# A fused attention and feed-forward kernel: loads of q and k in pairs, a new written-out order, and the norm's reciprocal root moved from VectorE to GpSimd

## The chip, the cores and the metric

One core of one Trainium2 chip runs the whole program. The metric is the device time in microseconds of one execution, the median over runs. The engines are TensorE (PE; its weight loads are listed apart as PEld), VectorE (DVE), ScalarE (ACT), GpSimd (POOL, which also makes the descriptors of the DMAs that it issues) and SyncE (SP, which here only issues DMAs). Matrix products land in eight PSUM banks of 128 x 512 fp32.

## The reference

Attention with a window of 128 keys and 4 sink keys over 4 batches, 8 heads, 768 positions, head size 64; then an RMS norm over the 512 features of each of the 3072 tokens and a SwiGLU feed-forward layer of width 1536.

```python
scores = (q @ k.T) / sqrt(64)             # per batch and head
keep   = is_sink | (0 <= i - j < 128)     # 4 sink keys, window of 128
a      = softmax(where(keep, scores, -1e9))
x      = (a @ v), heads side by side      # 3072 x 512
rms    = sqrt(mean(x * x, axis=-1) + 1e-6)
xn     = x / rms * rms_g
g      = xn @ w_gate                      # 512 x 1536
out    = ((g * sigmoid(g)) * (xn @ w_val)) @ w_out
```

Inputs and output are fp32; the kernel computes in bf16 with fp32 sums.

## The kernel before

The 3072 tokens are 24 blocks of 128, numbered g = 0 to 23, six to a batch (t = g mod 6). Six groups G of four blocks go through the feed-forward layer.

**One block of attention.** POOL issues three loads for each block (q, k, v: `load_bf16`, L353, and `load_v`, L357), which cast to bf16 on the way; only q and k of block 0 come as fp32 through SP and are cast by ACT (L349). For blocks 0 to 7 PE transposes q and k (`pe_t`, L445, four 128-column transposes for each), and DVE or ACT copies the result into the tile `qkT` (`copy_t`, L452); from block 8 on SP does it with a transposing DMA (`dma_t`, L459). Scores are computed transposed, keys on partitions: a block's keys against the queries of the same block (n = 0) and of the next (n = 1). Blocks 0, 1, 2, 3 and the first of each batch use `scores` (L485): eight products of 256 columns into four banks, one for each half of the heads and each of `u`; blocks 0 and 1 do it in two parts of eight products of 128 columns (`SPLIT`). Blocks with t = 1 to 4 from block 4 on use `tri_scores` (L563, 24 products of 64 x 64 tiles), the last of a batch `scores_last` (L501). Blocks 0 and 1 are masked on PE by a product that writes a bias first (`mask_bias`, L467), later ones after the exponential, on DVE (L547, L584, L520) or, from block 16, on POOL (L597, L526). ACT takes the exponentials (L536, L572, L512). `av` (L606 to L621) multiplies with the values; a column of ones in `V16` gives the denominators. `normal` (L660, L661, DVE) divides, `square` (L669, ACT) sums the squares into `ms`.

**The norm.** `rms` (DVE) turns `ms` into the reciprocal root by six operations on 128 x 1 (L676, L680 and four at L689) and then scales the block by it and by the gain `gb` (L693), giving `xr`. The constant C3 that these six leave over is folded into `gb` (`scale_gb`, L431). `xr` is transposed into `xnt`, for blocks 0 to 7 by PE (`pe_x`, L708) and a copy (L714), later by an SP DMA (`dma_x`, L720).

**The feed-forward layer.** A chunk is one bank of `g` (L975 with wg) and one of `u` (L975 with wv), `tanh` on ACT (L982), `silu` (L988) and `hidden` (L998) on DVE. Group 0 has chunks of 128 tokens and four 128-wide pieces of d_ff, groups 1 and 2 of 256 tokens, the rest of 512. `project` (L1008) multiplies with w_out, ACT evacuates (L1016), SP stores (L1020). The last 128 rows are done by `project_end` (L1028) in two pieces, 384 and 128 columns; ACT evacuates and stores the first, DVE and SP the second.

**What sets the order.** Nothing is decided at run time. Every operation is handed to a plan under a number; the table `ORDER` lists the numbers for each engine, `TURNS` how the engines' lists interleave as the program is written down, and `BANKS` the PSUM bank for each product. Each engine then works through its list strictly in that order and waits where an input is missing. Priorities and due times in the calls (`prio`, `gate_of`, `LOAD_LEAD`) were used to make the tables and do nothing any more once they stand. 56 small products of zeros (`warm`, L421) are part of PE's list; all stand within its first 22 us. POOL keeps at most eight loads in flight: each issue waits until the eighth load before it has landed.

Below, g(G, f, c) and u(G, f, c) name the two halves of the chunk of group G that starts at piece f and token c; s.3 stands for the scores of block 3, av.3 for its product with the values, xr.3, ms.3, qT.3, kT.3 for its tiles.

Of the kernel before, what the change touches and what calls it, by code (L numbers as in the profile page):

```python
# [9 lines left out]
ALU = mybir.AluOpType  # L10
# [9 lines left out]
C3 = -5.0 / 16.0  # L20
T1 = 2.5258847276
TP = T1 - 4.2
TQ = 7.0 / T1
# [48 lines left out]
140 138 114 151 122 152 124 143 154 119 156 157 117 111 142 173 171 153 127 133 118 163  # L72
135 169 149 112 198 123 174 179 167 165 186 136 141 148 200 134 125 129 184 164 121 161
120 131 202 128 139 221 146 203 208 240 144 162 223 213 190 215 155 137 115 194 113 225
596 145 147 159 132 150 597 166 160 242 219 232 126 234 158 130 611 116 601 612 616 238
602 631 617 606 626 621 607 259 622 244 627 632 636 251 277 253 261 637 263 196 666 656
279 661 257 281 269 651 271 646 294 641 319 657 647 286 658 288 296 652 642 321 298 662
275 663 323 671 292 305 672 307 681 667 676 331 329 668 673 677 311 691 339 315 686 682
696 354 687 697 335 347 345 692 701 369 706 317 360 362 707 702 384 736 375 716 711 737
721 377 738 712 726 398 717 727 389 741 391 742 417 731 722 751 746 743 752 405 407 747  # L80
732 761 756 762 753 757 776 425 748 766 423 771 767 772 777 432 781 816 782 817 447 791
796 438 440 792 806 786 818 797 787 801 462 821 455 811 802 453 807 822 471 473 823 493
831 826 812 827 832 484 828 486 500 512 833 502 836 846 837 851 847 861 841 876 842 852
862 521 866 856 871 857 523 881 867 877 872 891 530 886 882 887 896 892 897 548 898 921
541 922 539 926 936 916 906 566 907 927 559 908 557 937 946 584 917 575 931 941 947 589
577 932 951 942 901 952 956 966 902 991 903 986 971 591 961 911 987 912 972 967 913 957
992 996 1001 962 1006 1002 1007 1021 1011 993 981 997 976 1012 1016 988 1022 982 1026
983 1036 1031 1017 1046 1037 1061 1032 1051 977 1052 1047 1066 978 1027 1041 1056 1042
1057 1067 1058 1062 1068 1063 1071 1074
""",  # L90
    "ACT": """
24 20 22 199 177 175 178 176 182 180 181 183 168 188 222 204-206 211 207 212 209 191 210
217 226 228 227 229 195 598 220 236 603 613 618 608 243 633 628 260 623 245 247 246 248
638 278 262 255 264-267 197 280 282 284 653 273 320 648 643 295 297 659 290 322 299 301
300 302 276 324 325 293 326 327 309 664 678 669 683 674 333 312 693 340 316 341 688 342
343 698 355-357 336 358 703 370 371 708 372 318 373 349 385 364 387 718 713 723 739 379
399 401 400 402 728 418 419 733 420 393 421 409 763 758 778 768 754 773 744 749 427 433
414 783 434-436 448 449 793 450 798 451 442 808 788 819 803 463-466 813 457 824 480 475
482 494 496 497 495 513 488 514 515 504 834 838 516 848 843 853 829 863 868 858 878 873
525 883 531-533 893 509 888 534 899 923 549-551 928 552 938 543 567-569 918 570 585 587  # L100
933 943 948 561 953 579 958 909 904 968 593 963 914 973 1008 1003 994 998 1013 1028 1023
989 1038 1018 1033 984 1053 1048 1043 979 1069 1059 1064 1072 1073
""",
    "DVE": """
0 2 7 1 3 6 11 10 14 172 170 13 12 187 4 185 193 201 189 192 241 224 214 216 314 218 230
231 233 235 599 237 600 239 604 605 614 5 619 615 620 609 634 610 629 624 625 630 249
250 252 254 639 640 256 268 258 635 270 283 285 272 654 274 649 644 287 289 650 655 413
645 291 303 313 304 306 308 328 310 332 679 330 684 680 334 694 689 685 344 699 690 700
346 348 695 359 704 361 363 709 374 710 705 350 719 386 376 714 378 724 715 388 365 720
390 404 729 392 380 730 403 725 508 422 408 734 406 735 394 764 410 759 765 760 426 412  # L110
769 424 779 774 770 428 775 784 780 785 437 794 439 441 795 452 809 789 799 800 790 443
804 456 805 454 810 814 472 474 458 476 815 498 485 499 487 501 503 489 507 505 849 839
840 844 850 854 855 845 864 522 869 865 859 524 860 879 870 880 874 875 884 526 885 894
889 890 895 924 540 925 542 929 939 919 560 930 558 544 920 576 934 590 940 935 944 949
945 578 562 950 954 955 959 580 592 969 594 970 960 964 974 975 1009 965 1004 1010 999
1000 1014 1005 1015 1029 1024 1025 1019 1020 1034 1039 1040 1035 1049 1054 1055 1050
1030 1044 1045 1075
""",
    "POOL": """
25 8 9 26-28 31 34 30 32 37 35 29 38 33 39 41 42 40 43 45 47 44 48 46 49 36 50 53 57 52  # L120
54 51 56 63 62 60 55 58 64 61 59 65-99 467 469 468 470 481 100 483 101-108 517 520 109
518 519 535 538 537 536 110 553 555 554 571 573 556 572 588 586 574
""",
    "SP": """
19 21 23 16 15 18 17 337 352 338 353 367 660 382 368 383 396 415 397 416 430 675 351 445
366 431 460 446 381 670 665 478 740 395 479 411 492 745 461 510 491 429 755 511 528 444
459 750 477 506 564 582 546 529 565 490 820 547 835 527 830 583 825 545 563 581 595 915
905 910 900 995 990 980 985 1070 1060 1065 1076
# [3 lines left out]
ASDDSDGDPDPSPDPPPPPGPPPGPDPGPPDDPGAGPPPPADGPPPPGPPSPDPSADPGSDPSPGAAAPAGPAPPDAPPGPPAPDPAP  # L132
PPPADPGPDAGPPDPPDGAPPGPAPPAGDPAPAPDGADAPDGPAPPPADPAGPDAPADAGPPPPAPADGAPADGPPPPPAPPDPGPPD
DPAGPDPAGPDPGAPDDGPDGPDADGDPDGPADADPGAADPGPGDPADGAPDPGADAPGADADPGDPAPPDAPPDADAPGDPPADAGP
AAGPAPDAPPDPADPDAPGDAPDDGDPAPGDPPGSAAPGADAPGDPDGPPPDAGDAPGDADPPGADPAGDSAPPAGASPADPADSADP
PPGADAPGPSADDPGASAPGDPGSAPPGDPSADGAPDASDAPPDADPAGPPSAAADPAADPADPDAPAGADPGADPPDAPPADDPDGS
PDAPASAGDPPAPAGDSPADAPADDPPAGSADPPDASDPAGPADPSDDPGAPDDPADAPDGSDPDGPAGAPADSAPPADSDPPDGPDS
PDAGASPAAPDASGDPADSPDSDPGSPPPDDPSDGPDADPAPADPSDPSPDPSPDDAPDPDAPADPADAPDADAPDPDPASAPDASAP
DSADPADPDPASAPASADPAPPDASDPDAPSDASPADPDADPDPDPDAPASAPPDASADPAGPDGPGDPDGAPDPDPDPDAPAAGPSA
DGPAASGPADSPAGDPPGDDPGPPDGPDAAGPPDAGADPAGPAAGDPADAGPGPDSPGDPDASGPDGAADSPDAPDSDPPDSPDAPDS  # L140
ADPDSAPPDSDPSDAPDASPADDPDPDPADAPAAPDASADPADSPGSDGPDGSPGPGPAPAPADPAPDADPADAPDAGAPDGPGPAAP
AAPPADGDPPDGPDGDGPPAAPDSPGDPGAGPDAPPDPDPDPDAADPADPDDPAPAADPSDPDPDDPAAPPSPDDPAAPDPPSPPDPA
PSDSDSPASDPDPPPAAPDDPDPDPPAAPSDPDPAPDDPDPPPPAAPDADPSDPAAPDPDPAAPDDPDPDAPADPDPDPDPPDPAAPD
SPSDPPPPPAAPSASSPAADS
"""
BANKS = """
# [9 lines left out]
def kernel(  # L156
# [44 lines left out]
    POOL_MASK_FROM = 16  # L201
    X_DMA_FROM = 8
    QK_DMA_FROM = 8
    LD = 16
    GATE_FROM = 8
    LOAD_LEAD = 10
    LEAD_FROM = 10
# [222 lines left out]
    def scale_gb():  # L430
        nc.scalar.mul(gb, BANK.pop(("gb",)), C3)  # L431
# [709 lines left out]
```

## Time and profile before

| | before |
|---|---|
| median of 3 runs | 241.71 us (241.56 to 242.35) |
| profiled execution, first to last instruction | 241.9 us |
| its distance to the median of the runs | 0.2 us above |
| PE busy | 231.3 us (96%) |
| DVE busy | 187.4 us (77%) |
| ACT busy | 122.8 us (51%) |
| POOL busy | 89.2 us (37%) |
| granted PE clock | 1.00 |
| DMA packets | 113741, of which 103857 under 512 B |
| the queue of POOL's loads | 13.90 MB, 79.3% of the 16 DMA engines' time |

The profile is of one execution; PE is busy nearly throughout, and its products overlap in the pipeline, so a single product's duration (0.2 to 0.4 us) is longer than the time from one start to the next. The text takes the time from start to start wherever work is summed. The idle time of an engine is listed with what ended it.

### The profile page before, as it was taken

Reading aid. Unit: us, or ns where it says so; the run is one execution under the profiler, and the core shown is the slowest. Engines: PE = TensorE matmul, PEld = TensorE weight load, DVE = VectorE, ACT = ScalarE, POOL = GpSimd, SP = SyncE. Lnnn points to the kernel's source line nnn. Section 1 sums busy time; section 2 is a strip of 40 time slices with the busy share of each in tenths; the row PEclk is TensorE's granted clock in tenths of the full one; section 3 lists DMA queues with packets and bytes.
Section 4 is the critical chain, followed back from the end, with each engine's and each line's share of the span. In section 5 each row is a group of like instructions: output and inputs, shape, how many; then the busy total and the mean of one; then the engine's idle time right before and its main releaser. Section 6 shows DMA issues by size and latency. Waiting matters only on the chain.

```text
span 241.9 us, 5897 instructions
## 1 busy us (share of the span) xinstructions
PE 231.3 (96%) x2329; PEld 147.6 (61%) x2354; DVE 187.4 (77%) x478; ACT 122.8 (51%) x267; POOL 89.2 (37%) x116
## 2 busy tenths in 40 slices
PE   7889999999879999999999999999999999999995
PEld 5568986876668776777876644445554444444443
DVE  3599989989979999999898989994569946537520
ACT  4776368667766574337654464454543321233112
POOL 8985894597526554000004982022540000000000
PEclk9999999999999999999999999999999999999999
DMA  9999999999999999999601999527010114101024
GB/s 128 143 183 195 182 178 194 162 143 139 137 151 152 138 143 154 132 233 156 126 2 24 119 150 123 131 70 128 3 23 0 32 36 173 43 0 47 0 87 173
DMA packets 113741, 27.42 MB, mean 113 GB/s; under 512 B 103857, under 2 KB 110769, under 8 KB 113714
## 3 DMA queue, kind: packets, MB, share of 16 engines
q0 software_dynamic: 81760, 13.90, 79.3%
q1 hardware_dynamic: 31810, 12.95, 29.8%
q8 instruction: 18, 0.29, 0.5%
q10 hardware_dynamic: 144, 0.20, 0.2%
q14 instruction: 9, 0.07, 0.1%
HBM read 28.35 MB, written 6.29 MB: 143 GB/s over the span
## 4 chain that ended last, share of the span: by engine, by line
PE 67%; DMA 20%; POOL 6%; issue 2%; DVE 2%; SPq 2%; POOLq 0%
PE v L975 20%; PE o L1008 20%; PE g L975 18%; DMA wo<-in_moe_w_out_dram 5%; DMA qkT<-q 4%; DMA wv<-in_moe_w_val_dram 4%; DMA wg<-in_moe_w_gate_dram 3%; DMA q<-in_q_dram 3%; POOL v L357 2%; SPq L459 2%; PE s L563 2%; PE av L621 2%; POOL k L353 1%; PE av L616 1%; PE o_last L1028 1%
## 5 line engine op out<-in xcount | busy, mean ns | idle before, releaser
L975 PE MATMUL v<-xnt,wv 128*128 128x128 bf16 (+2 forms) x527 | 72.2, 282 | 0.4 <-DMA wv<-in_moe_w_val_dram 0.2
L975 PE MATMUL g<-xnt,wg 128*128 128x128 bf16 (+2 forms) x521 | 71.3, 281 | 0.4
L1008 PE MATMUL o<-wo,hT 128*128 128x512 bf16 x259 | 65.3, 379 | 1.1 <-issue 0.5
L982 ACT ACTIVATE th<-g 128x512 bf16<-128x512 f32 x72 | 41.7, 599 | 48.4 <-PE g L975 48.2
L988 DVE SCALAR_TENSOR_TENSOR p<-th,g 128x512 bf16<-128x512 bf16 x72 | 48.1, 682 | 18.9 <-ACT th L982 18.7
L975 PEld LDWEIGHTS <-wv 128*128 128x128 bf16 x528 | 43.3, 98 | 21.3 <-DMA wv<-in_moe_w_val_dram 0.6
L998 DVE TENSOR_TENSOR hT<-p,v 128x512 bf16<-128x512 bf16 x72 | 48.1, 682 | 9.3 <-PE v L975 7.8
L975 PEld LDWEIGHTS <-wg 128*128 128x128 bf16 x528 | 42.8, 98 | 19.3 <-issue 1.0
L1008 PEld LDWEIGHTS <-hT 128*128 128x128 bf16 x276 | 25.4, 98 | 26.5 <-issue 0.2
L597 POOL TENSOR_SCALAR_AFFINE_SELECT e<-e 128x512 bf16<-128x512 bf16 x20 | 12.7, 656 | 54.4 <-ACT e L572 53.0
L572 ACT ACTIVATE e<-s 128x384 bf16<-128x384 f32 x52 | 23.1, 495 | 12.5 <-PE s L563 12.5
L1016 ACT ACTIVATE osb<-o 128x512 f32<-128x512 f32 x23 | 13.4, 597 | 21.8 <-PE o L1008 18.0
L357 POOL DMA_DIRECT2D v<-in_v_dram x24 | 21.3, 888 | 8.5 <-DMA q<-in_q_dram 3.8
L353 POOL DMA_DIRECT2D q<-in_q_dram x23 | 20.4, 891 | 9.9 <-DMA k<-in_k_dram 6.7
L353 POOL DMA_DIRECT2D k<-in_k_dram x23 | 20.4, 889 | 9.1 <-DMA v<-in_v_dram 4.5
L669 ACT ACTIVATE sq<-x 128x512 bf16<-128x512 bf16 x24 | 15.1, 631 | 14.8 <-DVE x L661 14.5
L661 DVE TENSOR_TENSOR x<-av,rden 128x256 bf16<-128x256 f32 x48 | 20.4, 424 | 1.7
L693 DVE SCALAR_TENSOR_TENSOR xr<-x,r,gb 128x512 bf16<-128x512 bf16 x24 | 18.7, 778 | 0.8
L621 PE MATMUL av<-v,e 128*128 128x65 bf16 x192 | 16.4, 193 | 0.3 <-DMA v<-in_v_dram 0.3
L536 ACT ACTIVATE e<-s 128x512 bf16<-128x512 f32 (+1 forms) x36 | 15.1, 519 | 1.6 <-PE s L485 1.5
L616 PE MATMUL av<-v,e 128*128 128x65 bf16 x160 | 14.8, 193 | 0.0
L621 PEld LDWEIGHTS <-e 128*128 128x128 bf16 x192 | 12.7, 97 | 2.8 <-DVE e L547 0.4
(78 smaller groups left out, 192.6 us busy)
## 6 DMA issues: line engine op xcount, KB each, us to landing
out_dram<-osb SPq DMA_DIRECT2D x23, 256.0 KB, 2.2
v<-in_v_dram POOLq DMA_DIRECT2D x24, 128.0 KB, 8.9
q<-in_q_dram POOLq DMA_DIRECT2D x23, 128.0 KB, 8.1
k<-in_k_dram POOLq DMA_DIRECT2D x23, 128.0 KB, 9.6
wo<-in_moe_w_out_dram POOLq DMA_DIRECT2D x2, 768.0 KB, 11.3
wg<-in_moe_w_gate_dram POOLq DMA_DIRECT2D x5, 256.0 KB, 8.0
wv<-in_moe_w_val_dram POOLq DMA_DIRECT2D x5, 256.0 KB, 8.9
stage<-in_k_dram SPq DMA_DIRECT2D x1, 256.0 KB, 3.0
```

The lines of the kernel that those rows point to most:

```text
L353: nc.gpsimd.dma_start(out=T[name, g], in_=block_of(src, g))
L357: nc.gpsimd.dma_start(out=V16[b][:, t, :, 0:D], in_=block_of(v, g))
L572: nc.scalar.activation(out=e_tile(g)[:, x:x + 2, 0:TW], in_=BANK.pop(("s", g, u, hi))[:, 0:2 * TW].rearrange("p (j c) -> p j c", c=TW), fu ...
L616: nc.tensor.matmul(out=dest, lhsT=T["e", g - 1][:, x, P:2 * P], rhs=V16[b][:, t - 1, h, :], start=(t == 1), stop=False, skip_group_check=True,
L621: nc.tensor.matmul(out=dest, lhsT=T["e", g][:, x, 0:P], rhs=V16[b][:, t, h, :], start=(t == 0), stop=True, skip_group_check=True,)
L661: nc.vector.tensor_tensor(out=T["x16", g][:, 4 * u:4 * u + 4, :], in0=pvv[:, :, 0:D], in1=rden.unsqueeze(2).to_broadcast((P, 4, D)), op=AL ...
L693: nc.vector.scalar_tensor_tensor(out=T["xr", g], in0=T.pop(("x16", g)).rearrange("p h d -> p (h d)"), scalar=r[:, 3:4], in1=gb, op0=ALU.mu ...
L975: nc.tensor.matmul(out=ps[:, i * n:(i + 1) * n], lhsT=w_sb[:, kt, ft * P:(ft + 1) * P], rhs=T["xnt", G][:, kt, cols], start=(kt == 0), sto ...
L982: nc.scalar.activation(out=T["th", key], in_=BANK[("g", key)], func=ACT.Tanh, scale=0.5,)
L988: nc.vector.scalar_tensor_tensor(out=T["p1", key], in0=T.pop(("th", key)), scalar=1.0, in1=BANK.pop(("g", key)), op0=ALU.add, op1=ALU.mult,)
L998: nc.vector.tensor_tensor(out=T[hk][:, i:i + n, cols], in0=T.pop(("p1", key)).rearrange("p (n c) -> p n c", n=n), in1=BANK.pop(("v", key)) ...
L1008: nc.tensor.matmul(out=BANK[("o", G, tb)], lhsT=T["h", G, ft // 4][:, ft % 4, tb * P:(tb + 1) * P], rhs=wo[:, ft, :], start=(ft == 0), sto ...
```

## The change

**Pairs.** q and k of blocks 2 and 3, 4 and 5, 6 and 7 are each loaded by one DMA (`load_pair`) in which a partition holds two neighbouring positions, so that each run in memory is twice as long; six issues are saved. `pe_pair` transposes such a tile by sixteen products with 64 output partitions each, in two column halves of the array, in place of twice four with 128; `copy_pair` interleaves the two positions again as it copies to `qkT`. Two loads of weights of one piece each become one of two pieces, for each of wg and wv.

**Scores by n.** `scores`, `exps`, `mask_bias` and `mask_dve` now have a bank for each (n, half of the heads) in place of (u, half). All of these blocks use sixteen products of 128 columns, and four exponentials of 128 x 512 in place of, in blocks 0 and 1, eight of 128 x 256.

**The norm.** The six DVE operations are gone. `rsqrt` on POOL adds 1e-6 and raises to the power -0.5 with a constant tile `half`; DVE then does only the scaling. C3 leaves `gb`, whose evacuation becomes a copy.

**New tables.** `ORDER`, `TURNS` and `BANKS` are new, made with `LOAD_LEAD` 6 and `LEAD_FROM` 8 (10 and 10 before) and without the gates; `LD`, the number of buffers for loads, is 12 (16). In PE's new list the bias for g stands ahead of all attention (`gbm`, before k of block 0 is cast on ACT), scores of blocks 0 to 4 come before the first chunk g(0,0,0) (before: of blocks 0 to 2), pairs of blocks 2 to 5 are loaded ahead of all weights, and 29 of the 56 `warm` products stand early; the other 27 stand after the last real product. Of the last 128 rows the piece of 128 columns is now computed first and that of 384 last. On POOL each `rsqrt` stands between loads, in the order in which the loads and the masks are listed.

```diff
+    PAIRS = (2, 4, 6)
-    LOADS = "q-1 k-1 v-0 w-0-2 v-1 qkv-2 qkv-3 w-2-4 w-4-6 w-6-8 w-8-9 w-9-10 w-10-12 qkv-4 wo-0-6 qkv-5 wo-6-12 qkv-6 qkv-8 qkv-7"
+    LOADS = "q-1 k-1 v-0 w-0-2 v-1 QK-2 v-2 v-3 w-2-4 w-4-6 w-6-8 w-8-10 w-10-12 QK-4 v-4 wo-0-6 v-5 wo-6-12 QK-6 v-6 v-7"
...
+    def load_pair(name, src, g):
+        b, t = divmod(g, NT)
+        T[name, g] = ld.tile([P, H, 2, D], BF16, name=f"{name}2", bufs=2)
+        nc.gpsimd.dma_start(
+            out=T[name, g].rearrange("p h j d -> p h (j d)"),
+            in_=src[b, :, t * P:(t + 2) * P, :].rearrange("h (p j) d -> p h (j d)", j=2),
+        )
...
-        nc.scalar.mul(gb, BANK.pop(("gb",)), C3)
+        nc.scalar.copy(out=gb, in_=BANK.pop(("gb",)))
...
+    def pe_pair(n, g):
...
+        for hp in range(HP):
+            for j in range(2):
+                for hi in range(2):
+                    nc.tensor.transpose(
+                        out=ps[hi * D:(hi + 1) * D, hp, j, :], in_=src[:, 2 * hp + hi, j, :],
+                        identity=ident, tile_position=(0, hi * D),
+                    )
+
+    def copy_pair(n, g, i, eng):
...
+        ps = BANK[n, g].bitcast(BF16).rearrange("p (x j c) -> p x c j", x=HP, j=2)
...
+    def scores(g, n):
...
+        for hp in range(HP):
             for hi in range(2):
...
                 nc.tensor.matmul(
+                    out=BANK[slot][:, hp * P:(hp + 1) * P],
+                    lhsT=qkT[pr, 1, hp, t * P:(t + 1) * P],
+                    rhs=qkT[pr, 0, hp, (t + n) * P:(t + n + 1) * P],
...
+    def rsqrt(g):
+        T["rs", g] = small.tile([P, 1], FP32, name="rs")
+        m = small.tile([P, 1], FP32, name="m")
+        nc.gpsimd.tensor_scalar(
+            out=m, in0=T.pop(("ms", g)), scalar1=1e-6, scalar2=None, op0=ALU.add,
+        )
+        nc.gpsimd.tensor_tensor(out=T["rs", g], in0=m, in1=half, op=ALU.pow)
+
     def rms(g):
-        m = small.tile([P, 1], FP32, name="m")
-        nc.vector.tensor_scalar(
-            out=m, in0=T.pop(("ms", g)), scalar1=1e-6, scalar2=None, op0=ALU.add,
-        )
...
-        for o, i0, s0, s1, op0 in (
...
-            nc.vector.tensor_scalar(
-                out=r[:, o:o + 1], in0=i0, scalar1=s0, scalar2=s1, op0=op0, op1=ALU.mult,
-            )
         T["xr", g] = xpool.tile([P, DM], BF16, name="xr")
         nc.vector.scalar_tensor_tensor(
             out=T["xr", g], in0=T.pop(("x16", g)).rearrange("p h d -> p (h d)"),
-            scalar=r[:, 3:4], in1=gb, op0=ALU.mult, op1=ALU.mult,
+            scalar=T.pop(("rs", g)), in1=gb, op0=ALU.mult, op1=ALU.mult,
         )
```

## The prediction

> **What bounds the kernel now.** I read the page first, then PE's busy time by stretch, who PE waits for, and the timelines of the head and the tail.
>
> ```profile
> PE 231.3 (96%) x2329; PEld 147.6 (61%) x2354; DVE 187.4 (77%) x478; ACT 122.8 (51%) x267; POOL 89.2 (37%) x116
> ```
> ```profile
> 20.00:30.00 10.00, 9.98 (x181) 9.63 (x180) 9.45 (x23) 4.22 (x9) 7.43 (x9) 1.00 1.60 189
> ...
> 60.00:80.00 20.00, 17.89 (x266) 13.97 (x264) 17.53 (x45) 12.94 (x31) 10.49 (x13) 1.00 2.00 144
> ...
> sum 216.00, PE 211.66 PEld 134.16 DVE 174.47 ACT 107.73 POOL 72.20; mean PE 23.52 PEld 14.91 DVE 19.39 ACT 11.97 POOL 8.02
> ```
> ```profile
> PE s L563 <- DMA qkT<-q: 1.3, 1, 1.3
> PE s L563 <- DMA qkT<-k: 0.8, 1, 0.8
> ```
>
> The second fence is busy time by stretch (length, then PE, PEld, DVE, ACT, POOL, clock, DMA); its sum covers 20 to 236 us, in which PE stands idle for 216.0 - 211.7 = 4.3 us. Half of that is the third fence: two waits, at 65 and 70 us, for transposed q and k. Waits for v (0.3) and wv (0.2) add 0.5; 1.7 us are crumbs. PE waits nowhere there for DVE, busy as it is. So the kernel is a head in which PE lacks work, then a stream of products, then a tail; only what shortens the head, the stream or its waits counts.
>
> ```profile
> 16.06 0.61 PE L485 MATMUL s<-qkT 64*128 64x256 bf16 x8
> 16.60 1.07 PE L975 MATMUL g<-xnt,wg 128*128 128x128 bf16 x16
> ...
> 20.95 1.06 PE L975 MATMUL g<-xnt,wg 128*128 128x128 bf16 x16
> ...
> 42.19 0.40 PE L501 MATMUL s<-qkT 64*128 64x128 bf16 x8
> 42.52 0.28 PE L606 MATMUL av<-vsk,esk 128*128 128x260 bf16 x1
> ```
> ```profile
> 3.85 0.62 ACT L349 CAST k<-stage 128x512 bf16<-128x512 f32 x1 [1.76 <-DMA stage<-in_k_dram]
> ...
> 7.31 2.32 ACT L536 ACTIVATE e<-s 128x256 bf16<-128x256 f32 x8 [0.47 <-PE s L485]
> ...
> 53.24 2.07 ACT L536 ACTIVATE e<-s 128x512 bf16<-128x512 f32 x4
> ```
> ```profile
> 236.15 2.78 PE L1028 MATMUL o_last<-wo,hT 128*128 128x384 bf16 x24
> 238.30 0.49 ACT L1043 ACTIVATE last<-o_last 128x384 f32<-128x384 f32 x1 [1.24 <-PE o_last L1028]
> 238.82 0.37 ACTq L1046 DMA_DIRECT2D out_dram<-last  x1
> 238.97 0.29 DVE L1039 TENSOR_SCALAR last<-o_last 128x128 f32<-128x128 f32 x1 [7.11 <-PE o_last L1028]
> 239.28 0.33 SPq L1046 DMA_DIRECT2D out_dram<-last  x1
> ```
>
> From start to start, eight score products of 256 columns take 0.54 us and eight of 128 take 0.33. The first chunk half starts at 16.6; from 20.95 on the stream is dense. PE ends at 238.94, the span 2.96 later.
>
> **The sum is made on PE.** Before: 20.95 + W + 4.3 idle + 2.96 = 241.9, so W, the work after 20.95, is 213.7 us. After: the start of g(0,0,0), plus the work then left, plus idle, plus tail.
>
> *Work left.* Before, g(0,0,0) and u(0,0,0) are done by 20.95; after they are not: +1.8 (a half is 0.90, 21.90 to 22.80). After, s.3 (0.54), s.4 (0.48, 38.34 to 38.82) and transposes for four tensors (0.23 each, 40.78 to 41.00) are done already: -1.9. Late scores by n, blocks 6, 12 and 18: sixteen products of 128 for eight of 256, 2 x 0.33 - 0.54 = 0.12 each, +0.4. Pairs of block 6: sixteen transposes into column halves for eight at 0.057. No row has this form; the nearest, the four L742 products into 32 columns, take 0.055 for 256 columns where the array undivided needs about 0.11, so halves overlap. From 0.03 each (all overlap, no loss against 0.46) to 0.057 (none, +0.45 for each of two); I take +0.1 each, the L742 row being nearest. Work left: 213.7 + 1.8 - 1.9 + 0.4 + 0.2 = 214.2.
>
> *Head.* ACT sets it. `gb` now goes ahead of the k cast: PE's L428 (1.05) and ACT's L431 (0.69) push it from 3.85 by about 1.9. From cast to first exponential took 3.46 before, which gives 9.2, and 9.6 with the pair of q queued ahead of q of block 1. Then, in the new ACT list up to kT.4, which s.4 needs: 13 exponentials at 0.51 (2.07 / 4), two squares at 0.72, two copies at 0.53, one sink exponential at 0.3: 9.4, so kT.4 at 19.0. Meanwhile DVE must do xr.1, qT.5, n.2 and xt.0; with the `rsqrt` between ms.1 (17.5) and xr.1 at 0.5 us this ends at 20.5. `copy_pair` reads PSUM with a stride; bounds from 0.42 (the DVE copy row, L452) to 0.68 (a DVE operation on 512 without speed-up, L988), +0.3 on the path. Start of g(0,0,0): 20.8. Loads bound it lower: before, the weights of the first u landed at 18.1 with 4.1 MB read up to them (eight loads of 256 KB, four of 512); now the second piece of wg, which g(0,0,0) needs, stands behind 4.35 MB, at the 185 GB/s of 12 to 20 us 1.4 later, 19.5. They don't set it. The other pairs' transposes lie in PE's idle time here (11 us of work by 20.8): nothing, or 0.4 each of two on the path.
>
> *`rsqrt`.* The trace has no power on POOL. Rows near it are a memset of 128x1, 0.10, and the select on 128x128, 0.30: two operations, 0.2 to 0.6; I take 0.5, being nearer to the select. It could even shorten the path, as 1.2 us of six DVE operations go. These six rows sum to 28.8 us of DVE in all. Nobody waits for it, so they are worth nothing by themselves; they cover the masks and `hidden` that now crowd 20 to 50 us. Behind each `rsqrt` on POOL stand loads: rs.5 stands ahead of wo, rs.6 ahead of k of block 10 and v of block 8. Six pairs and two weights save 8 issues of 0.75 to 0.88 (6.8 us of POOL), and v of block 8 would land at about 65, its use is at about 69: covered by 4 us, late beyond that.
>
> *Idle.* The transposes' wait (2.1) should go: q of block 9 is now issued at about 45 (47.27 before) and POOL then pauses for rs.6, so that SP's transposes run without loads beside them. The 0.5 for v and wv goes, too. New: PE's eight banks are emptied by DVE, whose list between 20 and 50 leaves almost no gap; 0 to 4 us, I take 1.0. Idle 1.7 + 1.0 = 2.7.
>
> *Tail.* The 384 columns come last: ACT's 0.49 + 0.37 for DVE's 0.29 + 0.33, and a store of 192 KB for one of 64: +0.3, 3.3 in all. The 27 products of zeros at the end, 27 x 0.055 = 1.5 us, lie beside it; without this cover they cost those 1.5.
>
> Sum: 20.8 + 214.2 + 2.7 + 3.3 = 241.0, against its own 241.9. The median stands 0.2 below the profiled span, so **240.8 us**.
>
> **Rivals.** *A: GpSimd is slow, and slower than before is the result.* The L597 selects take 624 ns at best and 852 at worst beside DVE, the DVE scaling L693 750 and once 1136: the two hold each other up. If each POOL operation waits out a DVE one (0.68) or the power itself is several times my 0.5, rs.0 and rs.1, both in front of DVE operations that all later copies queue behind, cost 1.4 each: 20.8 becomes 23.6, time **243.6**. It decides when an `rsqrt` takes over 1 us from ms to rs. Against it: POOL is the less busy engine, and most selects run at 0.65. The Trainium skill, "SBUF — State Buffer", on the port pair that DVE and GpSimd share, says that a DVE instruction with two SBUF inputs and a GpSimd instruction that reads SBUF exclude each other, the later waiting in full. That rule speaks for A; the 852 and 1136 agree, the median of 651 does not show it often.
>
> *B: the banks.* If DVE can't empty them between 25 and 47 us, or column halves don't overlap (+0.9 for block 6, +0.8 on the path), idle grows by 1.9: **242.7**. For: DVE is 94% busy at 20 to 30 already. Against: its list is 1.2 us shorter for each block.
>
> *C: the head is set by loads alone.* g(0,0,0) at 19.5: **239.5**. For: first exponentials of 512 replace pairs of 256, and ACT idles for some 4 us in the head before. Against: the new list puts 13 exponentials ahead of kT.4.
>
> **How the numbers follow.** Forecast 45% (faster 33, same 12, since its own spread is about 240.0 to 241.6), A 20% (slower), B 20% (slower 13, same 7), C 15% (faster). A difference under 0.3% (0.7 us) can't be told from none here. Together: faster 0.48, same 0.19, slower 0.33. The range goes down to C without the 1.0 of new idle, 238.5, and up to A with a little of the 4 us of bank waits, 244.2.
>
> **What would show it.** Right: first chunk half at 20 to 21.5; PE idle after it under 4 us with no wait for qkT at 60 to 80; POOL's two rows at L698 and L701 summing to under 0.6 us each time; six DVE rows gone and DVE at about 160 us; the span's end 3 to 3.5 us after PE's last 384-column product. Wrong: PE waiting for xr or kT past 22 us, waits of g and u for DVE between 25 and 50, or a load late behind an `rsqrt`.

## The result and the profile after

| | before | after |
|---|---|---|
| median | 241.87 us (241.56 to 242.35, 4 runs) | 248.24 us (248.17 to 249.23, 4 runs) |
| ratio to before, 95% interval | | 1.0269 (1.0247 to 1.0290): slower |
| profiled execution, first to last instruction | 241.9 us | 246.5 us |
| DVE busy, POOL busy | 187.4, 89.2 us | 164.9, 106.0 us |

Forecast were 240.8 us in a range of 238.5 to 244.2: the sign and the range were wrong. Ratios in this document compare undisturbed executions only, so that a ratio can differ a little from the quotient of two medians.

The page after, the lines of busy time and of the granted PE clock (40 slices of the span, in tenths):

```profile
PE 236.7 (96%) x2442; PEld 151.0 (61%) x2442; DVE 164.9 (67%) x341; ACT 117.7 (48%) x253; POOL 106.0 (43%) x156
PEclk9998999999999999999999999999999999999999
```

Busy time by stretch (length, then PE, PEld, DVE, ACT, POOL, clock, DMA share, GB/s):

```profile
20.00:30.00 10.00, 8.37 (x150) 7.26 (x145) 8.44 (x19) 7.13 (x18) 7.79 (x12) 0.83 1.52 173
30.00:40.00 10.00, 10.00 (x199) 9.93 (x196) 8.95 (x21) 3.63 (x8) 3.98 (x6) 1.00 1.10 114
40.00:50.00 10.00, 8.88 (x174) 8.53 (x171) 8.62 (x17) 6.12 (x13) 9.08 (x13) 1.00 1.44 113
...
60.00:80.00 20.00, 20.00 (x235) 12.57 (x233) 15.20 (x34) 10.86 (x28) 14.19 (x19) 1.00 1.91 140
...
100.00:150.00 50.00, 48.44 (x500) 32.26 (x497) 36.59 (x73) 24.13 (x55) 21.59 (x32) 1.00 1.21 129
```

PE's waits after, in total, times, longest:

```profile
PE g L991 <- DMA xnt<-xr: 1.5, 2, 0.9
PE av L627 <- DVE vsk L746: 1.5, 1, 1.5
PE s L514 <- DVE qkT L478: 1.2, 2, 0.8
PE q L469 <- DMA q<-in_q_dram: 1.1, 1, 1.1
```

Both waits for transposed q and k at 60 to 80 us are gone, and PE never waits for a bank between 30 and 40. In their place are waits for xnt, for vsk, for the strided copies and for the pair q of block 6. The clock of 0.83 says that PE ran at half rate for 3.4 of the 10 us from 20 to 30; the rows below from 22.2 on, where products take about double, agree.

The head, from the timeline:

```profile
3.86 2.04 PE L441 MATMUL gb<-grow,ones 1*128 1x512 f32 x2 [0.61 <-DMA grow<-in_moe_rms_g_dram]
...
9.94 1.06 PE L469 MATMUL q<-ident,q 128*64 128x128 bf16 x16
...
11.04 0.59 ACT L478 COPY qkT<-q 128x512 bf16<-128x512 bf16 x1 [2.01 <-PE q L469]
...
11.58 1.08 ACT L561 ACTIVATE e<-s 128x512 bf16<-128x512 f32 x2
...
19.93 0.19 ACT L690 ACTIVATION_READ_ACCUMULATOR sq<-x 128x1 f32 x1
...
20.52 0.57 POOL L701 TENSOR_TENSOR rs<-m,half 128x1 f32<-128x1 f32 x1
...
20.98 0.59 ACT L478 COPY qkT<-k 128x512 bf16<-128x512 bf16 x1
21.07 0.70 DVE L746 TENSOR_TENSOR vsk<-vsink,headm 128x520 bf16<-128x520 f32 x1 [1.01 <-DMA vsink<-in_v_dram]
21.45 1.59 ACT L561 ACTIVATE e<-s 128x512 bf16<-128x512 f32 x3
21.69 0.74 DVE L705 SCALAR_TENSOR_TENSOR xr<-x,rs,gb 128x512 bf16<-128x512 bf16 x1
21.83 0.28 PE L627 MATMUL av<-vsk,esk 128*128 128x260 bf16 x1 [1.46 <-DVE vsk L746]
...
23.18 1.10 PE L584 MATMUL s<-qkT 64*64 64x192 bf16 x24 [0.17 <-ACT e L561]
...
23.61 0.41 DVE L726 COPY xnt<-x 128x512 bf16<-128x512 bf16 x1
...
24.61 2.44 PE L991 MATMUL g<-xnt,wg 128*128 128x128 bf16 x32
```

The first chunk half starts at 24.61; the sum had 20.8. Three things stand in these lines. ACT waits 2.0 us for the pair q.2 before it may start its first exponential (11.58), since the copy of the pair stands ahead of it in ACT's list; s.0.0, which stands behind the pair in PE's list, was itself done only at 11.54. vsk, whose source was loaded early in the kernel before, waits for SP's four small loads into `vsink`, and av.2 and xr.1 wait behind it. And s.4 (L584) comes only after the three exponentials at 21.45, which free its banks.

The tail is as forecast, 3.4 us from PE's last product of 384 columns to the end of the span:

```profile
240.35 2.78 PE L1044 MATMUL o_last<-wo,hT 128*128 128x128 bf16 x24
...
242.97 1.67 PE L434 MATMUL warm<-zeros 128*128 128x128 bf16 x27
243.17 0.49 ACT L1059 ACTIVATE last<-o_last 128x384 f32<-128x384 f32 x1 [1.91 <-PE o_last L1044]
243.69 0.37 ACTq L1062 DMA_DIRECT2D out_dram<-last  x1
```

One reading of numbers has to be mended here. The four executions after have times of 248.22, 248.25, 248.17 and 249.23 and spans of 246.5, 246.5, 246.4 and 247.5: the time is 1.7 us above the span in each. So it is for the kernel before where it was run beside the experiments (242.12 beside 240.4, 241.83 beside 240.1, and so on). The page of before, with its span of 241.9, therefore shows an execution some 1.7 us longer than the usual one, and not a span that equals the time.

### The profile page after: what moved, and what is told of

Its sections match the earlier page's. It is cut to its first block, busy times and chain, and to the rows that moved or that the text cites. A ratio compares the mean times of both kernels' runs of the same rounds, so it can differ in the third digit from the quotient of the medians.

```text
span 246.5 us, 6031 instructions
## 1 busy us (share of the span) xinstructions
PE 236.7 (96%) x2442; PEld 151.0 (61%) x2442; DVE 164.9 (67%) x341; ACT 117.7 (48%) x253; POOL 106.0 (43%) x156
## 4 chain that ended last, share of the span: by engine, by line
PE 58%; issue 13%; POOL 12%; DMA 9%; DVE 5%; ACT 1%; SPq 1%; POOLq 0%; DVEq 0%; ACTq 0%
PE o L1024 18%; PE v L991 16%; PE g L991 16%; POOL rs L701 3%; POOL q L352 3%; DMA k<-in_k_dram 2%; DMA q<-in_q_dram 2%; POOL k L352 2%; DMA xnt<-xr 2%; DMA vsink<-in_v_dram 2%; POOL m L698 2%; POOL v L364 2%; PE s L584 1%; PE o_last L1044 1%; PE av L642 1%
## 5 line engine op out<-in xcount | busy, mean ns | idle before, releaser
L991 PE MATMUL v<-xnt,wv 128*128 128x128 bf16 (+2 forms) x528 | 71.3, 282 | 0.1
L1024 PE MATMUL o<-wo,hT 128*128 128x512 bf16 x276 | 66.7, 379 | 0.0
L991 PEld LDWEIGHTS <-wv 128*128 128x128 bf16 x528 | 42.6, 98 | 18.9 <-issue 0.6
L698 POOL TENSOR_SCALAR m<-ms 128x1 f32<-128x1 f32 x24 | 7.4, 306 | 74.1 <-ACT sq L690 72.5
L705 DVE SCALAR_TENSOR_TENSOR xr<-x,rs,gb 128x512 bf16<-128x512 bf16 x24 | 19.1, 797 | 12.9 <-POOL rs L701 12.9
L690 ACT ACTIVATE sq<-x 128x512 bf16<-128x512 bf16 x24 | 15.1, 631 | 22.2 <-DVE x L682 21.3
L618 POOL TENSOR_SCALAR_AFFINE_SELECT e<-e 128x512 bf16<-128x512 bf16 x20 | 14.0, 717 | 9.6 <-ACT e L593 9.4
L561 ACT ACTIVATE e<-s 128x512 bf16<-128x512 f32 x28 | 15.0, 604 | 4.4 <-PE s L514 4.4
L642 PE MATMUL av<-v,e 128*128 128x65 bf16 x192 | 16.9, 194 | 0.2 <-POOL e L618 0.2
L352 POOL DMA_DIRECT2D k<-in_k_dram x17 | 15.6, 921 | 0.8 <-POOLq L1138 0.8
L352 POOL DMA_DIRECT2D q<-in_q_dram x17 | 15.6, 916 | 0.0
```

Of the source, the lines that this page charges most:

```text
L352: nc.gpsimd.dma_start(out=T[name, g], in_=block_of(src, g))
L642: nc.tensor.matmul(out=dest, lhsT=T["e", g][:, x, 0:P], rhs=V16[b][:, t, h, :], start=(t == 0), stop=True, skip_group_check=True,)
L690: nc.scalar.activation(out=sq, in_=T["x16", g].rearrange("p h d -> p (h d)"), func=ACT.Square, scale=1.0 / math.sqrt(DM), accum_out=T["ms" ...
L705: nc.vector.scalar_tensor_tensor(out=T["xr", g], in0=T.pop(("x16", g)).rearrange("p h d -> p (h d)"), scalar=T.pop(("rs", g)), in1=gb, op0 ...
L991: nc.tensor.matmul(out=ps[:, i * n:(i + 1) * n], lhsT=w_sb[:, kt, ft * P:(ft + 1) * P], rhs=T["xnt", G][:, kt, cols], start=(kt == 0), sto ...
L1024: nc.tensor.matmul(out=BANK[("o", G, tb)], lhsT=T["h", G, ft // 4][:, ft % 4, tb * P:(tb + 1) * P], rhs=wo[:, ft, :], start=(ft == 0), sto ...
```

## The experiments

The theory after the first comparison: the time is lost in the head (order of the lists, vsink, clock) and in loads that stand on POOL behind a power that waits for `ms`, not in the power itself. The rivals: the power is the whole loss (rival A of the prediction); the 27 products of zeros at the end are no longer covered; the clock. Unless said otherwise a kernel is the changed one with one edit. The lists are those of `ORDER`, written with the names of their operations.

**e1_no_tail.** The 27 last products of zeros taken away.

```diff
     def warm(i):
+        if i in TAIL:
+            return
         ps = bank(("warm", i))
```

> The changed kernel without the 27 products of zeros that stand last in PE's list (nothing else computed is left out). Theory: after the last real product they run on past the last store; the changed kernel's time stands 1.7 us above its profiled span in every run (248.22 against 246.5), and 27 x 0.062 is 1.7: the time falls to 246.5 and meets the span. Rival: they lie beside the tail, as the prediction had it, and the gap has another cause: 248.2, gap unchanged.

The four executions took 246.42, 248.17, 250.38 and 252.05 us; the ratio of 1.0211 (1.0163 to 1.0259) rests on the first two. The gap stayed 1.7 us in all four (246.42 beside a span of 244.7, 252.05 beside 250.3), so these products are not its cause. That they lie beside the tail, as the prediction had it, is seen in the profile after: they end at 244.6, 1.9 us before the span does. The spread of the times is larger than the effect that was looked for, so they say nothing about these products.

**e2_vsink_early.**

```diff
-DVE: ... bias.1 masks ... ksk.0 vsink1 n.0.1 ...
+DVE: ... bias.1 vsink1 masks ... ksk.0 n.0.1 ...
```

> The changed kernel with the memset of vsink and SP's four loads into it moved up to where the kernel before has them (memset right behind the bias, loads right behind). Theory: DVE's vsk waits for these loads until 20.95 and holds up av.2, xr.1 and the copy of qT.5; without it xr.1 starts when rs.1 is there (21.1 instead of 21.69) and av.2 about 0.8 earlier, so g(0,0,0) starts at about 23.7 instead of 24.6 and the time is 247.3. Rival: another wait of the head (exponentials, kT.4) takes its place at once: g(0,0,0) within 0.2 of 24.6, time 248.2.

246.70 us, 1.0198 (1.0163 to 1.0234): 1.5 us by the medians, more than expected. In its profile g(0,0,0) starts at 22.96, in an execution whose products ran at full rate from about 8.5 us on (11.8 after) and whose pair's copy came 1.0 earlier; e7, whose lists are the same up to 30 us, has 23.76, the 23.7 of the theory, with the pair's copy where it is after. PE's wait for vsk fell from 1.5 to 0.5. The wait that then ends last is the one that the rival named:

```profile
PE s L584 <- ACT e L561: 1.3, 1, 1.3
```

**e3_dve_norm.** `rsqrt` does nothing, `rms` has the six VectorE operations of before again, `gb` is scaled by C3.

> The changed kernel with the six small VectorE operations back in place of the GpSimd power (gb scaled by their constant again), all else as changed. Theory: a norm's root costs 1.2 us of DVE instead of 0.9 of latency through POOL, no gain by itself, but POOL no longer stands waiting for ms with loads queued behind it: the wait for q of block 6 (1.1) goes and the head's loads come earlier; DVE is 28.8 us busier. About 247.0, g(0,0,0) within 0.5 of 24.6. Rival A of the prediction (the power and its waits are the whole loss): 243 or less. Rival: DVE has no room: 249.5.

261.96 us, 1.0817 (1.0793 to 1.0841): all expectations missed, the last one, no room on DVE, by 12 us in its own direction. The chain that ended last in this kernel, by engine:

```profile
PE 51%; DVE 36%; DMA 7%; issue 4%; ACT 1%; SPq 1%; DVEq 0%
```

In the new order six small DVE operations for each block lie on the path. Putting them back therefore says nothing of the price of the power, so e16 was made.

**e4_before_pow.** The kernel before, with the norm's root alone on POOL.

```diff
     def rms(g):
-        (six nc.vector.tensor_scalar)
+        nc.gpsimd.tensor_scalar(out=m, in0=T.pop(("ms", g)), scalar1=1e-6, scalar2=None, op0=ALU.add)
+        nc.gpsimd.tensor_tensor(out=rs, in0=m, in1=half, op=ALU.pow)
```

> The kernel before with the norm's root alone changed to the GpSimd power, its two POOL operations standing where the six VectorE operations stood in the joint order; loads, order and blocks of lead as before. Theory: the price of the power by itself is small, POOL's waits for ms push single loads by 2 to 3 us, of which one or two are not covered: 241.9 to 244, middle 243. Rival: free or a gain, since 28.8 us of DVE go: 241.0. Rival A: 245 or more.

244.12 us, 1.0079 (1.0053 to 1.0104): 1.9 us slower, in the expected range. 25 us of DVE fewer (161.9) bring nothing, POOL stands 44.4 us waiting for `ms`, and PE waits 2.0 for xr.

**e5_k_first.** On top of e2: the cast of k ahead of the copy of gb, block 0's k and mask ahead of block 1's.

```diff
-ACT: gb k.0 kT.1 qT.0 qT.2 x.0.0.1 ...
+ACT: k.0 gb kT.1 qT.0 qT.2 x.0.0.1 ...
-PE: gbm mb.1.1 kp.1 qp.0 mb.0.0 kp.0 qp.2 s.0.0 ...
+PE: gbm kp.0 mb.0.0 kp.1 qp.0 mb.1.1 s.0.0 qp.2 ...
```

> The changed kernel with the early vsink and, besides, the head's lists in another order: the cast of k ahead of the copy of gb on ACT, the transposes of k, block 0, and its mask products ahead of those of block 1, and s.0.0 ahead of the pair q.2. Theory: the first exponential starts at about 9.7 instead of 10.6 (11.58 without the early vsink), since kT.0 no longer stands behind gb; ACT's list to kT.4 carries this on, g(0,0,0) 1 us earlier than the 22.9 of the early vsink: 245.6. Rival: another wait of the head (a load, DVE's strided copies) ends last: 246.7 as with the early vsink alone.

246.35 us, 1.0177 (1.0153 to 1.0202): the rival, no difference from e2 that can be told. s.0.0 was done at 10.4, but the first exponential came at 12.01, because qT.2 stood ahead of it:

```profile
11.53 0.59 ACT L478 COPY qkT<-q 128x512 bf16<-128x512 bf16 x1 [2.23 <-PE q L469]
```

gb ahead of the k cast was not what held ACT up.

**e6_warm_head.** On top of e2: 29 products of zeros in PE's gaps between 14 and 22 us.

> The changed kernel with the early vsink and with 29 products of zeros more between 14 and 22 us where PE idles (7 ahead of s.2, 6 ahead of av.2.1, 16 behind av.2.0; 13 of them taken from the end of PE's list). Theory: the granted clock stays at 1.0 from 20 to 30 (0.83 before) and the 32 products of g(0,0,0) and g(0,0,128) take 1.8 instead of 3.4: 1.6 less, 245.1. Rival: the clock falls all the same, or the products delay av.2 and s.4 as much as they bring: 246.7.

249.85 us, 1.0319 (1.0279 to 1.0358): missed, 3 us slower than e2. The clock did stay at 1.0 from 20 to 30, but the products had to wait for banks themselves: the seven ahead of s.2 took 1.86 us, s.2 started at 16.48 (14.68 in e2; 0.7 of the difference was there before them) and g(0,0,0) at 25.73. Fillers that need a bank aren't free.

**e7_loads_first.** On top of e2.

```diff
-POOL: ... rs.3 wv8-9 wv10-11 k.6 rs.4 v.6 q.6 q.8 ...
+POOL: ... wv8-9 rs.3 wv10-11 k.6 v.6 q.6 rs.4 q.8 ...
```

> The changed kernel with the early vsink and, on POOL, two loads (v and the pair q of block 6) ahead of rs.4 and one (wv8-9) ahead of rs.3. Theory: these loads stand behind a power that waits 3.2 and 3.4 us for ms; issued first, the pair q.6 lands before PE needs it, PE's wait of 1.2 at 48 us goes: 245.5. Rival A: the norm's power becomes late instead (xr.4, xr.3 on DVE) and the gain is lost: 246.7 or more.

245.76 us (244.46 to 247.22), 1.0136 (1.0082 to 1.0189). Right on the mechanism: PE's wait for q.6 is gone and 40 to 50 us is filled (10.00 of 10.00). The gain is 0.9 by the medians, less than the spread: the profiled execution waits 3.0 us for xnt instead:

```profile
PE g L991 <- DMA xnt<-xr: 3.0, 3, 1.3
```

**e8_before_again.** The kernel before, for a second profile.

> The kernel before, unchanged, for a second profile. In the runs so far the device time stands 1.7 us above the profiled span for every kernel, the one before too (240.4 beside 242.1), while the span of the page that the prediction read was 241.9. Theory: that one execution was 1.5 to 2 us longer than usual, and its two waits for transposed q and k (2.1) are what was longer: in this profile they are under 0.5 and the span about 240.2. Rival: the waits are there in every execution, and something else differs.

Span 240.5 and time 242.18. Of the two waits for transposed q and k (2.1 us) one remains:

```profile
PE s L563 <- DMA qkT<-k: 0.7, 1, 0.7
```
```profile
100.00:150.00 50.00, 49.94 (x512) 33.36 (x511) 46.13 (x125) 27.39 (x60) 15.13 (x20) 1.00 1.14 119
```

The theory holds but for its figure (0.7, not under 0.5). Note the second fence for later: the kernel before loses nothing from 100 to 150 us. The page shows one thing more:

```profile
PE 233.8 (97%) x2354; PEld 148.6 (62%) x2354; DVE 187.2 (78%) x478; ACT 122.6 (51%) x267; POOL 89.3 (37%) x116
```

Here every load of weights (2354) has its product. The first page has 2329 products for the same 2354 loads: 25 products of 512 columns are missing from its records, and the gaps that they leave look like idle time of PE. From its dense start (21.52) to PE's last product, this execution idles 0.9 us.

**e9_q1_first.** On top of e5: q.1 loaded and transposed ahead of the pair, ACT's first two exponentials ahead of the pair's copy.

> The kernel of e5_k_first (early vsink, k cast first) with the load of q, block 1, ahead of the pair q.2 on POOL, its transposes ahead of the pair's on PE, and the pair's copy qT.2 behind the first two exponentials on ACT. In e5 s.0.0 was done at 10.4, but ACT stood at the copy of the pair, which PE transposed at 10.42 to 11.4, and the first exponential came at 12.01. Theory: the 256 KB pair in front of block 0's and block 1's exponentials sets the head: they now start at 10.4 to 10.6 and those of block 1 at 11.6 instead of 13.1, ACT is the full engine from there on, so g(0,0,0) comes 1.2 earlier than e5's 23.9: 245.1. Rival: the wait moves to DVE's strided copies or to k.2, 246.3 as before.

247.64 us, 1.0247 (1.0217 to 1.0276): missed, 1.3 slower than e5. The first two exponentials came at 10.55 as expected, but the pair was now transposed at 12.42 behind s.1.0, and its copy still stood ahead of all other exponentials:

```profile
13.10 0.59 ACT L478 COPY qkT<-q 128x512 bf16<-128x512 bf16 x1 [1.46 <-PE q L469]
13.59 1.58 ACT L561 ACTIVATE e<-s 128x512 bf16<-128x512 f32 x3
...
21.92 0.58 ACT L478 COPY qkT<-k 128x512 bf16<-128x512 bf16 x1
```

g(0,0,0) moved with it, from 23.91 to 25.00, and the time by the same 1.1 to 1.3. From the pair's copy to kT.4 ACT needs 8.8 here, with two exponentials fewer between them, and 9.3 to 9.9 in the changed kernel, e2, e5, e7, e15 and e16: ACT's list runs on from the pair's copy, not from gb.

**e10_q1_loads.** e9 with the loads of e7.

> e9_q1_first with the three loads of e7_loads_first ahead of rs.3 and rs.4. Theory: the two add up, PE's wait of 1.1 for the pair q.6 at 48 us goes: 1.0 below e9, 244.1 if e9 gives 245.1. Rival: PE waits for xnt take back what the earlier q.6 gives, as in two of the four executions of e7: equal to e9 in the median.

246.47 us, 1.0198 (1.0174 to 1.0221), 1.2 below e9: the theory's difference, on a base that was wrong. The wait for q.6 is gone again.

**e11_q1_lead.** e10 with the loads behind rs.7 moved up by one to two powers.

> e10_q1_loads with the loads behind rs.7 moved up by one to two powers on POOL and 13 buffers instead of 12. Theory: with six blocks of lead loads run beside SP's transposes from 100 to 180 us (the transposes of k land after 5.8 to 6.4 us, 2.4 in the kernel before), and PE waits 0.5 to 3.3 us there for xnt, another sum in every execution; with the loads earlier these waits fall under 0.5: 0.5 to 1.5 below e10, 243.2, and a narrower spread. Rival: the loads push rs.5 to rs.7 and the transposes at 60 to 80 us back: as e10 or above.

255.94 us, 1.0592 (1.0560 to 1.0623): missed by far. PE is busy for 16.66 of the 20 us from 60 to 80 and for 46.40 from 100 to 150:

```profile
PE ss L754 <- DMA qkT<-q: 3.3, 2, 2.1
PE v L991 <- DVE x L682: 2.6, 1, 2.6
```

PE waits for transposed q and for DVE at places where e10 does not; which of the moved loads does it was not traced. That the shorter lead makes the waits for xnt was not shown; this run speaks neither for a cure by it nor for another cause.

**e12_gap_warm.** 16 of the last 27 products of zeros moved to the front, 8 ahead of gb, 8 ahead of kp.1.

> The changed kernel with 16 of the 27 products of zeros at the end of PE's list moved to the front: 8 ahead of gb (PE idles 0.61 there) and 8 ahead of the transposes of k, block 1 (0.3 idle). Theory: the clock rises when PE has been busy without a gap for some 3.4 us; with the gaps filled it rises by 5 to 8 us instead of 12, the products of 5 to 12 us take half, the first exponential comes 1 us earlier (10.5 instead of 11.58), g(0,0,0) too: 247.2. Rival: loads set the first exponential, 248.2; or the products themselves delay gb and the mask products: 249.

249.75 us, 1.0332 (1.0280 to 1.0385): slower, as the second rival said. The products delay what stands behind them: k of block 1 is transposed at 8.47 (7.27 after). PE has no gap of 0.1 us from 1.04 to 9.9 us, and yet gb and the products of 7 to 9 us run at half rate; only those from about 10 on are full:

```profile
1.04 3.06 PE L434 MATMUL warm<-zeros 128*128 128x128 bf16 x27 [1.04 <-DVE zeros L282]
4.04 2.07 PE L441 MATMUL gb<-grow,ones 1*128 1x512 f32 x2
...
8.47 0.63 PE L458 MATMUL k<-ident,k 128*128 128x128 bf16 x4
...
10.42 0.39 PE L458 MATMUL k<-ident,k 128*128 128x128 bf16 x4
```

**e13_together.** e7 with the 16 products of e12 in front, and g(0,0,0) ahead of s.4.

> The changed kernel with the early vsink, the three loads ahead of rs.3 and rs.4, the 16 products of zeros of e12_gap_warm, and g(0,0,0) ahead of s.4 on PE, with the copy xt.0 that it needs ahead of xr.1 on DVE. In e7 s.4 waits 1.34 for the banks of block 3's exponentials, with g(0,0,0) behind it. Theory: g(0,0,0) fills this wait (0.9 of work) and the clock rises earlier (up to 1.0): 1.0 to 1.9 below e7's 245.8, 244.3. Rival: xr.1 or av.2 is late by xt.0 and the wait stands elsewhere: 245.8.

246.65 us (244.85 to 247.73), 1.0182 (1.0127 to 1.0236): no better than e7. With the same front as e12 the clock was up by 4.7 us in the profiled execution:

```profile
4.09 1.32 PE L441 MATMUL gb<-grow,ones 1*128 1x512 f32 x2
...
9.12 0.59 ACT L478 COPY qkT<-q 128x512 bf16<-128x512 bf16 x1 [0.61 <-PE q L469]
9.60 1.09 ACT L561 ACTIVATE e<-s 128x512 bf16<-128x512 f32 x2
...
20.90 1.05 PE L991 MATMUL g<-xnt,wg 128*128 128x128 bf16 x16 [1.37 <-ACT e L561]
```

So the moment of the rise isn't set by these gaps. What it is worth in the head shows here: in e12, with PE's list the same up to there, the pair's copy came at 11.41 and the first exponential at 11.89, 2.3 us later. And g(0,0,0) itself now waited 1.4, for the bank that block 3's last exponentials free.

**e14_before_cold.** The kernel before without its first 15 products of zeros.

> The kernel before without its first 15 products of zeros. Theory: PE starts at 3.3 instead of 1.33, the clock rises 2 us later or more (at 7 to 11 us instead of 4.7 to 7.4), the head's first products take double, and the time is 0.5 to 1.5 above the kernel before: 243.0. Rival: the head of the kernel before is set by loads, the clock there doesn't matter: 242.0.

241.73 us (10 runs), 1.0002 (0.9984 to 1.0021): the rival's time. PE starts at 3.30 instead of 1.33, and nothing is lost. But the clock did not rise later by it: PE is at full rate from about 7.3 us, as in e8 with all products in place, and the stream is dense from 21.41 (21.52 in e8, 20.95 in the first page, where the rise came by 4.7). So the 15 products bring nothing; that a late clock costs the kernel before nothing is not shown.

**e15_early_g.** e7 with g(0,0,0) ahead of s.4 in a bank that is free, and xt.0 ahead of xr.1.

```diff
-PE: ... av.2.0 s.4.0 xp.1 g(0,0,0) ...
+PE: ... av.2.0 g(0,0,0) s.4.0 xp.1 ...
-DVE: ... vsk.0 xr.1 qT.5 n.2.0 xt.0 ...
+DVE: ... vsk.0 xt.0 xr.1 qT.5 n.2.0 ...
```

> The kernel of e7_loads_first (early vsink, three loads ahead of rs.3 and rs.4) with g(0,0,0) ahead of s.4 on PE, xt.0 ahead of xr.1 on DVE, and banks 2 and 4 exchanged from there on, so that g(0,0,0) takes the bank that xt.0 frees. Theory: g(0,0,0) runs while s.4 waits for its banks (1.3), the head is 0.9 shorter: 244.9 against e7's 245.8. Rival: xt.0 ahead of xr.1 delays xr.1 and the block behind it by as much, or the gain is taken back in the waits for xnt: 245.8.

245.50 us (243.81 to 246.98), 1.0134 (1.0082 to 1.0185). The head does what was meant: g(0,0,0) at 20.42, s.4 behind it waits 0.4 instead of 1.3, PE is busy for 8.40 of 20 to 30 (7.69 in e7). The time doesn't show it: PE is busy for 47.58 of 100 to 150 and 49.15 of 150 to 200, with 1.8 of waits for xnt. That is the rival, whose second part has the gain taken back there.

**e16_no_root.** The norm's root left out, VectorE scales by a constant column.

```diff
     def rsqrt(g):
-        nc.gpsimd.tensor_scalar(...)
-        nc.gpsimd.tensor_tensor(out=T["rs", g], in0=m, in1=half, op=ALU.pow)
+        T.pop(("ms", g))
...
-            scalar=T.pop(("rs", g)), in1=gb, op0=ALU.mult, op1=ALU.mult,
+            scalar=half, in1=gb, op0=ALU.mult, op1=ALU.mult,
```

> The changed kernel without the norm's root: the two POOL operations are left out and VectorE scales by a constant column, so that neither POOL nor xr waits for ms (the squares on ACT stay; the output lacks the norm). It bounds what the root through POOL costs with all its waits. Rival A of the prediction (the power and its waits are the loss): back to 242 to 243. Theory: the head is set by ACT's list from the pair q.2 on and by vsink, so only the wait for q.6 (1.1), some of the waits for xnt (1.5) and 0.5 in the head go: 246.0, and g(0,0,0) within 0.6 of 24.6.

246.37 us (244.15 to 247.81), 1.0145 (1.0065 to 1.0224), where 246.0 was expected; rival A's 242 to 243 lies below the interval. Without any power, and with POOL's loads flowing (182 GB/s from 40 to 50 us, 113 in the changed kernel), the kernel is still 1.5% slower than before:

```profile
40.00:50.00 10.00, 10.00 (x195) 9.80 (x192) 9.60 (x20) 5.82 (x13) 5.58 (x7) 1.00 1.71 182
...
100.00:150.00 50.00, 48.30 (x489) 31.89 (x496) 37.34 (x77) 25.25 (x57) 13.28 (x17) 1.00 0.89 97
```

By the ratios (1.0269 and 1.0145) the power with all its waits is worth 3.0 us of a loss of 6.5, and 0.6 to 5.4 with the two intervals taken at their ends; by the medians it is 1.9 of 6.4. e4 has 1.9 for the kernel before. So a loss of 1.6 us or more stands without any power, but whether the power is the larger or the smaller part is not settled. g(0,0,0) starts at 23.37, 1.2 earlier, of which 0.8 was there already at the pair's copy (10.23 against 11.04), ahead of any power.

## Why the prediction was wrong, by its own steps

The sum was start of g(0,0,0) + work left + idle + tail - 0.2. Measured in the profile after: 24.6 + 215.4 + 3.1 + 3.4 = 246.5, and + 1.7 for the time. Of the error of 7.4 us 3.8 are in the first term, 1.2 in the second, 0.4 in the third, 0.1 in the fourth and 1.9 in the last.

**Head, 20.8 for 24.6 (+3.8): the step that failed.** The sum's path ran over the first exponential, ACT's list up to ms.1, the root, and DVE's operations from xr.1 to xt.0. Along it ms.1 was there at 20.1 for 17.5 (+2.6), the root took 1.0 for 0.5 (+0.5), xr.1 then waited for vsk (+0.6), DVE's operations took 2.3 for 2.5 (-0.2), and g(0,0,0) came 0.6 after xt.0 where 0.3 were allowed (+0.3). ACT's list itself was priced well: up to the end of kT.4 9.4 us were forecast, and it took 9.9 (11.58 to 21.45), of which 0.56 is a wait for s.1.
- *The start, 9.6 for 11.58.* I let gb push the k cast and gave the pair q.2 0.4. But ACT takes its list in order, and the copy of the pair stands ahead of the first exponential; the pair was transposed at 9.94, in products at half rate. In e5 neither gb nor s.0.0 was in the way any more and the exponentials still waited for the pair's copy; in e9 all but the first two did, and the time followed them. The products of the head were priced at full rate, as in the page before, where it came by 4.7 us. With the rise at 4.7 (e13), 8.5 (e2) and 11.8 (after), and PE's real products in the same order up to there, the first exponential came at 9.60, 10.52 and 11.58. The forecast's 9.6 is that of an early rise; what brings one about no run here shows.
- *The end, 1.8 for 3.2 from kT.4 on (21.45 to 24.61).* The memset of vsink, late in DVE's list, was not in the sum at all. Without this wait g(0,0,0) starts 0.85 earlier (e7, 23.76), and the time was 1.5 lower in e2, part of which can be the clock. I read the move of each load on POOL, and not those on SP. And I took kT.4 for the last thing that s.4 needs. It needs banks as well, which three more exponentials free (1.6 us); e2 and e7 show this wait bare (1.3), e15 takes most of it away. s.4 and the transposes behind it then ran at half rate, 1.43 us against 1.00 in e7.

**Work left, 214.2 for 215.4.** The base W was mis-sized, and with it the idle time. The first page lacks 25 products, and W counted their gaps as crumbs of idle time. In e8, which has them all, W is 240.5 - 21.52 - 0.9 - 3.0 = 215.1 in place of 213.7, so 1.4 of the 1.7 us of crumbs was work. With it the term is 215.6, close to the 215.4, in which 0.6 is the clock: the 32 products from 24.61 took 2.4 us in place of 1.8. All four executions after have a mean clock of 0.986 to 0.993, most of the executions before 1.0. The transposes into column halves were priced right: sixteen take 0.57 us (16.45 to 17.02), 0.036 each, which is the 0.1 more for each tensor that was put in.

**`rsqrt`, 0.5 for 0.8.** The two rows, minimum, median and maximum in ns:

```profile
L698 POOL TENSOR_SCALAR m<-ms x24: 220/221/895, 16.0 to 196.6; 128x1 f32<-128x1 f32 x24
L701 POOL TENSOR_TENSOR rs<-m,half x24: 567/570/724, 16.3 to 196.9; 128x1 f32<-128x1 f32 x24
```

0.22 + 0.57 = 0.79, outside my 0.2 to 0.6; the 128x128 select that I took as the nearest row (0.30) costs about half of this power. The larger omission was the wait: I asked whether loads behind an `rsqrt` would land in time, and not how long POOL would stand in front of it. It stands 72.5 us in all:

```profile
40.68 0.38 POOL L698 TENSOR_SCALAR m<-ms 128x1 f32<-128x1 f32 x1 [3.41 <-ACT sq L690]
...
42.64 0.89 POOL L357 DMA_DIRECT2D q<-in_q_dram  x1
...
48.32 0.64 PE L469 MATMUL q<-ident,q 128*64 128x128 bf16 x16 [1.11 <-DMA q<-in_q_dram]
```

Rival A was thus right that GpSimd makes it slower, but it looked at the wrong thing, the duration in front of DVE. From the start of the addition to the end of the power it took over 1 us in 6 of 24 cases (1.55 at most), and 0.88 in rs.0 and rs.1, on which the rival put its cost. What the wait in front of POOL's loads and the root are worth together is 0.6 to 5.4 us (e16). The sentence of the Trainium skill that spoke for it ("SBUF — State Buffer", on the shared port pair) agrees with the trace: the five longest additions (0.38 to 0.90) each end within 0.1 us after a DVE operation with two SBUF inputs. One of them:

```profile
25.25 0.77 DVE L570 TENSOR_TENSOR e<-e,masks 128x1024 bf16<-128x1024 bf16 x1
25.42 0.68 POOL L698 TENSOR_SCALAR m<-ms 128x1 f32<-128x1 f32 x1 [1.90 <-ACT sq L690]
```

It decides little: all 24 additions together took 2.1 us more than 24 times the shortest.

**Idle, 2.7 for 3.1, of other parts.** Of the 2.7 1.4 was work (above), so that 1.3 us of real idle time stood in the sum and 3.1 came. The qkT waits went as said, and the banks (rival B) cost nothing: 10.00 of 10.00 from 30 to 40. New are q.6 (1.1) and xnt (1.5). The cover of v.8, which I had doubted, held. But the 2.1 that I credited was a property of the one execution that I read: in the second profile of the kernel before it is 0.7.

Against that second profile (240.5) the 6.0 us of the span after are 3.1 in the start of the dense stream (24.61 for 21.52), 0.3 in work, 2.2 in waits and 0.4 in the tail.

**Tail, 3.3 for 3.4, its products of zeros covered: right.** DVE at about 160 (164.9): right.

**Time from span, -0.2 for +1.7.** With one page and three times nothing could tell a constant distance from an unusual execution; I took the two for equal, and should have put this 1.5 to 2 us into the range.

**What stays open.** e15, the best version tried, is still 3.4 us above the kernel before, and none beat it. The traces place much of it: from 100 to 200 us PE idles 2.0 us after, 3.3 in e15 and 0.1 in e8, most of it in waits for the transposes into xnt, another sum in every execution. POOL's power isn't their only cause (e16 idles 2.3 there, with 1.3 of these waits; its page and that of e15 lack 25 products, so that their idle time is somewhat less), and the lead of the loads could not be tested by itself (e11 changed too much). The transposes into xnt themselves land no later from 100 to 180 us than before (2.9 us in the median from issue, 3.4 in e8); those of k do (5.8 for 2.4). Why the clock falls at about 22 us I can't say either. It goes with the late vsink: where that stands late (after, e1, e3, e12, e16), 19 of 20 executions have a mean clock below 1.00, where it stands early 14 of 36. That PE's wait for vsk brings the fall is not shown; e10 waits only 0.5 us there and has 0.993 in all four.

## What to carry to other kernels

An engine with a strict list pays for the first item that isn't ready: when an order changes, look at what each engine's list holds ahead of the item that starts the path, memsets and small loads included, and count banks as inputs. An operation put on an engine that issues loads is priced by the time this engine stands waiting for its input, with the loads behind it, and not by its duration. And before a wait of one profiled execution is credited as a gain, see a second execution, and see whether the page has as many products as loads of weights: a missing record looks like idle time.

## What the hardware showed that was not expected

- The device time is 1.7 us above the span from first to last instruction (1.65 to 1.78) in every execution here for which both are on record, whatever stands at its end.
- PE's full rate came by 4.7 us (kernel before, first page; e13), at 7.3 (its second profile), 8.5 (e2), 10 (e12) and 11.8 us (after), with starts at 1.0 to 1.3 us. The page "TensorE: Matmul & The Clock Gate" of the Trainium skill, in "Part 1: The HAM clock gate", says that it rises after about 3.4 us of sustained work and falls after an idle window of that length. The rule does not hold here by itself: e12 worked for 9 us without a gap before it rose, and after, the rate fell at 22 us when no idle time of PE had been longer than 1.5 us. The length of the window agrees: the mean clocks of 0.993 and 0.986 would be one and two stretches of 3.4 us at half rate (0.007 x 246.5 = 1.7).
- A power on 128 x 1 takes GpSimd 0.57 us, an addition on the same 0.22, or up to 0.90.
- VectorE's copy out of PSUM with a stride of two elements takes 0.68 where the plain one takes 0.42; ScalarE takes 0.59 for both.
